# w3's last 64 columns placed directly in front of w4's first 64-row products

## The chip, the cores and the metric

The kernel runs on one core of one Trainium2 chip. The metric is the device time of one execution in microseconds (us), lower is better. A number given for a kernel is the median of several executions; the profile shows one execution, recorded by the hardware profiler.

A core has five engines that run side by side and wait for each other by semaphores: TensorE (PE in the profile; its weight loads are PEld), VectorE (DVE), ScalarE (ACT), GpSimd (POOL) and SyncE (SP, which issues most transfers). Matmul results go to PSUM, which has eight banks of 512 fp32 columns on 128 partitions; ACT and DVE take them out from there. SBUF is the working memory.

## What is computed

Two blocks work on the same input x of 2048 tokens by 640 features, and a gate per token mixes them. Cut to what matters:

```python
x = A_x
g = sigmoid((x * gate_w).sum(-1, keepdims=True))

# A: linear attention with 32 heads of 20, then wo
q, k, v = heads(x @ wqkv)
pq, pk = phi(q), phi(k)                  # phi(t) = where(t > 0, t + 1, exp(t)) + 1e-6
a = ((pq @ (pk.T @ v)) / (pq . sum(pk) + 1e-6)) @ wo

# B: two residual steps
h  = gelu(layernorm(x) @ w1)             # 640 -> 640
hs = shifted(h) @ w2                     # quarters shifted by 1, -1, 2, -2 tokens
x1 = x + hs
h2 = gelu(layernorm(x1) @ w3) @ w4       # 640 -> 1728 -> 640
b  = x1 + h2

out = g * a + (1 - g) * b
```

The change touches the last part, `gelu(layernorm(x1) @ w3) @ w4`. Its inner width is 1728 = 13 x 128 + 64: thirteen full tiles of 128 and a rest of 64.

## The kernel before

**Tiling.** The 2048 tokens are cut into 16 tiles of 128 (`NT`) and 4 chunks of 512 (`NCH`). For w3, a *group* (c, j) makes 128 of the inner columns (j = 0 to 12) for the 512 tokens of chunk c: `w3_group` (line 1076) runs five matmuls of 512 columns over the 640 features into one PSUM bank, and ACT writes the Gelu of it to `h2T`. `h2T` has two slots, so it holds two chunks. Full groups use the whole 128 x 128 array.

The 64 inner columns that are left are made by `w3_half(c)` (line 1085), called for c = 0 and c = 2, each for two chunks. Its weights have 64 columns, so two matmuls run side by side in the two column halves of the array (form 128*64 in the profile): five pairs, one for the even token tiles and one for the odd ones, into the two partition halves of one bank. One Gelu writes the result to `h2h`.

For w4, `w4_half(t)` (line 1146) opens the accumulation of the four token tiles of a chunk with the products of those 64 rows: the rows sit in the two partition halves of `h2h`, so here two matmuls run side by side in the two row halves of the array (form 64*128). There are four of 512 columns (line 1168) and, for the first three chunks, two of 256 (line 1172), which make the last 128 output columns in turned form. It takes six PSUM banks as three pairs and holds them. `w4_turned(t)` (line 1176) then adds the thirteen full tiles to the turned part (line 1188), ACT copies it to `mT`, and a transposing transfer brings it to `mtok`. `w4_tile(t)` (line 1195) adds the thirteen full tiles to the first 512 output columns of one token tile (line 1209), and DVE joins the result with the attention part into `x_tok`. `a_tile(t)` makes that attention part, ten matmuls on a pair of banks.

**The order of the work** is made when the program is built. The work is cut into items; each has a name, a duration, dependencies with a lag, and belongs to a stream, in which items keep their order (`_Items`, line 324). `run` takes, again and again, among the streams' next items whose dependencies are all emitted, the one that can start first by a rough simulation of its own; among equals, items of duration 0 go first (they hold no matmuls of the main line), then the one with the longest chain of durations and lags behind it. The chosen item's function emits its instructions to the queues of the engines, which run in that order on the chip. Waits are derived from what an instruction reads and writes, PSUM by whole banks. A bank is chosen by `bank()` (line 517) or a pair by `pair()` (line 534): the one that has been free longest in the simulation, never one that is held.

**Streams around the change.** Stream W3 holds the groups (c, j) in order of chunk and j. Group (1,7) to (1,10) each wait for an attention tile a(0) to a(3), and a(t) in turn waits for group (1,t+6), so that they alternate. The two items `("w3h", 0)` and `("w3h", 2)` stand in W3 ahead of group (1,11). They need the transposed, normalized x1 of tiles 4 to 7 and 12 to 15 (items t2). Stream W4 holds, for every chunk, w4h, w4x (the turned part, but for the last chunk) and four w4 items; t counts token tiles, so the chunks begin at t = 0, 4, 8 and 12. `("w4h", 0)` depends on a(0), a(3), on w3h(0) and on the last groups of chunks 0 and 1. From t = 4 on, a(t) depends on w4(t-4). Group (2,0) depends on a(7). `KFF` is 13, so `KFF - 2` is j = 11 and `KFF - 1` is j = 12.

On PE the stretch before the change thus runs: a(3), group (1,10), w3h(0), w3h(2), groups (1,11) and (1,12), w4h(0), w4x(0), w4(0), a(4), w4(1), a(5), and so on.

Of the kernel before, what the change touches and what calls it, by code (L numbers as in the profile page):

```python
# [18 lines left out]
KFF = F // 128  # L19
# [397 lines left out]
def _build(nc, A_x, A_wqkv, A_wo, B_w1, B_w2, B_w3, B_w4, gate_w, out, dbg=None, stop=None):  # L417
# [57 lines left out]
    w3 = pa.alloc("w3", [128, KD, F], BF16)  # L475
# [41 lines left out]
    def bank():  # L517
        best = None
        for k_ in range(nbanks[0]):
            b = (bank_rr[0] + k_) % nbanks[0]  # L520
            if b in bank_pend or b in bank_hold:
                continue
            lk = sch.locks.get(b)
            tfree = 0.0 if lk is None else sch.ev_time.get((lk[1].sem, lk[1].val), 1e18)
            if best is None or tfree < best[0]:
                best = (tfree, b)
        bank_rr[0] = best[1] + 1
        bank_pend.add(best[1])
        return best[1]
# [67 lines left out]
    def mm_group(out_ap, pairs, reads_extra=()):  # L597
        n = len(pairs)

        def fn(e, out_ap=out_ap, pairs=pairs, n=n):  # L600
            ins = None
            for i, (l, r) in enumerate(pairs):
                ins = e.matmul(out_ap, l, r, start=(i == 0), stop=(i == n - 1))  # L603
            return ins
        reads = [a for p in pairs for a in p] + list(reads_extra)
        return pe(fn, reads, [out_ap], cost=n * (max(nfree(pairs[0][1]), 24) * 0.4167 + 2.5))
# [39 lines left out]
    def activation(out_ap, in_ap, func, scale=1.0, bias=0.0, accum=None):  # L646
        rd = [in_ap] + [a for a in (scale, bias) if not isinstance(a, (int, float))]
        wr = [out_ap] + ([accum] if accum is not None else [])
        n = nfree(out_ap)
        cost = max(150.0, 100.0 + 0.833 * n + (70.0 if in_psum(in_ap) else 0.0)) + 45.0 * (len(rd) - 1)  # L650
        if accum is not None:
            cost += 91.0
        st_ = ACT_SET.get(func)
        if st_ is not None and st_ != sch.act_func:
            cost += 1290.0
            sch.act_func = st_
        if accum is not None:
            return act(lambda e: e.activation(out_ap, in_ap, func, bias=bias, scale=scale, accum_out=accum), rd, wr, cost=cost)  # L658
        return act(lambda e: e.activation(out_ap, in_ap, func, bias=bias, scale=scale), rd, wr, cost=cost)  # L659
# [103 lines left out]
    def tag_set(buf, sl, what):  # L763
        tags[(buf, sl)] = what

    def tag_chk(buf, sl, what):
        assert tags.get((buf, sl)) == what, ("stale ring slot", buf, sl, what, tags.get((buf, sl)))

    IT = _Items()
# [306 lines left out]
    def w3_group(c, j):  # L1076
        cols = slice(512 * c, 512 * (c + 1))
        sl = c % 2
        if j == 0:
            tag_set("h2T", sl, c)  # L1080
        b = bank()
        mm_group(ps[:, b, :], [(w3[:, k, 128 * j:128 * (j + 1)], xnT[:, k, cols]) for k in range(KD)])
        activation(h2T[:, sl, j, :], ps[:, b, :], ACTF.Gelu_apprx_tanh)

    def w3_half(c):
        b = bank()
        jobs = []
        for k in range(KD):
            xv = xnT[:, k, 512 * c:512 * (c + 2)].rearrange("p (n h q) -> p n h q", h=2, q=128)
            for par in range(2):  # L1090
                jobs.append((ps[64 * par:64 * par + 64, b, :], w3[:, k, 128 * KFF:F], xv[:, :, par, :], k == 0, k == KD - 1))

        def fn(e):
            ins = None
            for o, l, r, st, sp in jobs:
                ins = e.matmul(o, l, r, start=st, stop=sp)  # L1096
            return ins
        pe(fn, [w3[:, :, 128 * KFF:F], xnT[:, :, 512 * c:512 * (c + 2)]], [ps[:, b, :]], cost=KD * 218.0 + 200.0)
        activation(h2h[:, c:c + 2, :].rearrange("p c n -> p (c n)"), ps[:, b, :], ACTF.Gelu_apprx_tanh)
# [46 lines left out]
    def w4_half(t):  # L1146
        sl = (t // 4) % 2
        tag_chk("h2T", sl, t // 4)
        b0, b2, bt = pair(), pair(), pair()
        tiles = [((b0, b2)[i // 2] + i % 2, bt + i % 2, 128 * (i // 2)) for i in range(4)]  # L1150
        for i in range(4):
            w4_banks[t + i] = tiles[i]
        bank_hold.update((b0, b0 + 1, b2, b2 + 1, bt, bt + 1))

        turned = t < NT - 4

        def fn(e):
            ins = None
            for pr in range(2):
                for par, tail in ((0, False), (1, False)) if turned else ((0, False), (1, False), (0, True), (1, True)):  # L1160
                    rows = slice(64 * par, 64 * par + 64)
                    bm, bs, q0 = tiles[2 * pr + par]
                    l = h2h[rows, t // 4, 128 * pr:128 * (pr + 1)]
                    if tail:
                        ins = e.matmul(ps[:, bs, q0:q0 + 128], l, w4[rows, KFF, 512:D], start=(pr == 0), stop=False,
                                       skip_group_check=True)
                    else:
                        ins = e.matmul(ps[:, bm, :], l, w4[rows, KFF, 0:512], start=True, stop=False)  # L1168
            if turned:
                for par in range(2):  # L1170
                    rows = slice(64 * par, 64 * par + 64)
                    ins = e.matmul(ps[:, bt + par, 0:256], w4[rows, KFF, 512:D], h2h[rows, t // 4, :], start=True, stop=False)
            return ins
        pe(fn, [h2h[:, t // 4, :], w4[:, KFF, :]], [ps[:, b, :] for b in (b0, b0 + 1, b2, b2 + 1, bt, bt + 1)], cost=760.0)
# [66 lines left out]
    for c in range(NCH):  # L1241
        for j in range(KD):
            deps = [(("t1", u), 0.9) for u in range(4 * c, 4 * c + 4)] if j == 0 else []
# [6 lines left out]
    for t in range(NT):  # L1250
        c = t // 4
        deps = [(("w1", c, KD - 1), GEL)]
# [8 lines left out]
    for u in range(NT):  # L1261
        deps = [(("s2", u // 4), 3.2 + 0.9 * (u % 4))]
# [8 lines left out]
    for c in range(NCH):  # L1271
        for j in range(KFF):
            deps = []
            if c == 0 and j == 0:
                deps0 = [(("kvt", 1), 0.0), (("z", NT - 1), 1.5)]
            else:
                deps0 = []
            if j == 0:
                deps = deps0 + [(("t2", u), 0.9) for u in range(4 * c, 4 * c + 4)]
                deps.append((("w3load",), 0.0))  # L1280
                if c >= 2:
                    deps.append((("a", 4 * c - 1), 0.0))
            if c == 0 and j == 3:
                deps.append((("w2", NT - 1), 0.0))
            if c == 1 and 7 <= j <= 10:
                deps.append((("a", j - 7), 0.0))
            if c == 1 and j == KFF - 2:
                for c2 in (0, 2):
                    IT.add("W3", ("w3h", c2), 1.27, lambda c2=c2: w3_half(c2), [(("t2", u), 0.9) for u in range(4 * c2 + 4, 4 * c2 + 8)])
            IT.add("W3", ("w3", c, j), 1.08, lambda c=c, j=j: w3_group(c, j), deps)  # L1290
    for t in range(NT):
        deps = [(("zb",), 1.0), (("q", max(t, 2)), 2.0)]
        if t < 7:
# [11 lines left out]
    for t in range(NT):  # L1305
        c = t // 4
        deps = [(("qt", t), 3.0), (("w4load",), 0.0), (("m", 1), 1.0), (("mt",), 2.5)]
        if t >= 4:
            deps.append((("w4", t - 4), 0.3))
        else:  # L1310
            deps.append((("w3", 1, t + 6), 0.0))
        IT.add("AT", ("a", t), 1.33, lambda t=t: a_tile(t), deps)
        deps4 = [(("a", t), 0.0), (("w3h", c - c % 2), GEL), (("w3", c, KFF - 1), GEL)]
        if t % 4 == 0:
            deps4.append((("w3", min(c + 1, NCH - 1), KFF - 1), 0.0))
            if t == 0:
                deps4.append((("a", 3), 0.0))
        elif t + 3 < NT:
            deps4.append((("a", t + 3), 0.0))
        if t % 4 == 0:  # L1320
            IT.add("W4", ("w4h", t), 0.76, lambda t=t: w4_half(t), deps=deps4)
            if t < NT - 4:
                IT.add("W4", ("w4x", t), 2.84, lambda t=t: w4_turned(t), deps=deps4)
        IT.add("W4", ("w4", t), 2.8 if t < NT - 4 else 3.5, lambda t=t: w4_tile(t), deps=deps4)
        if t in OUT_AT:
            IT.add("OUT", ("out", t), 0.0, lambda t=t: out_tiles(OUT_AT[t], t + 1), deps=[(("w4", t), 0.0)])
# [48 lines left out]
```

## Time and profile before

| | us |
|---|---|
| median of 4 executions | 261.16 |
| lowest and highest of them | 260.34, 261.64 |
| the profiled execution's own time | 260.34 |
| its span, first to last instruction | 259.1 |
| PE busy in the span | 254.0 (98%) |
| DVE, ACT, POOL busy | 151.4, 109.7, 94.1 |
| PE in the stretch 112 to 148 | 35.79 of 36.00 |
| PE in the stretch 148 to 154, where the moved items are | 6.00 of 6.00 |
| PE in the stretch 154 to 256 | 101.42 of 102.00 |
| granted TensorE clock | 1.00 |

The profiler's span leaves out 1.2 us of the execution's own time. A matmul is recorded with its latency, so the records of consecutive matmuls overlap, and a PE that is busy the whole time can still start its matmuls further apart than it need; that is read from the starts, not from the busy time. Where a line of the profile names a helper (L603 for groups of matmuls, L659 for activations, L642 for DVE's multiply-adds), the tile names beside it tell what it works on: `xnT` with weights is a w3 group, `pqnT` an attention tile.

### The profile page before, as it was taken

The numbers are of one execution on the slowest core, as the hardware profiler recorded it, in microseconds if no ns is written. First come the engines' busy times: TensorE is split into PE (matmuls) and PEld (weight loads), VectorE is DVE, ScalarE is ACT, GpSimd is POOL, SyncE is SP. The second block draws the span as 40 slices with busy tenths as digits, with TensorE's granted clock in tenths as the row PEclk, the third lists the DMA queues.
The fourth block names the chain that finished last, engine by engine and source line by source line (L and its number), as shares of the span: only waits on it lengthen the run. The fifth ranks groups of instructions, "written<-read, shape, count | busy, mean of one in ns | idle before, by whom it ended". The sixth has DMA issues, their size and how long they took to land.

```text
span 259.1 us, 4106 instructions
## 1 busy us (share of the span) xinstructions
PE 254.0 (98%) x1571; PEld 130.9 (51%) x1600; DVE 151.4 (58%) x290; ACT 109.7 (42%) x223; POOL 94.1 (36%) x152
## 2 busy tenths in 40 slices
PE   8999999999999999999999999999999999999996
PEld 4555555554445554555444555444465444645453
DVE  2587877899914999999993403996004410044333
ACT  1396677751356866675854241005510045300000
POOL 5003995969952118767903201222002110012001
DMA  7665889572754798662835651115010020010211
GB/s 215 198 153 146 150 229 159 168 138 43 107 116 91 126 402 277 74 103 51 91 64 111 129 76 20 28 25 152 0 23 0 0 101 3 0 20 3 102 51 51
DMA packets 54308, 25.86 MB, mean 100 GB/s; under 512 B 45669, under 2 KB 52878, under 8 KB 54289
## 3 DMA queue, kind: packets, MB, share of 16 engines
q1 hardware_dynamic: 52112, 21.21, 36.7%
q0 software_dynamic: 1168, 3.28, 5.5%
q10 hardware_dynamic: 1008, 1.11, 1.3%
q8 instruction: 12, 0.20, 0.4%
q14 instruction: 8, 0.06, 0.1%
HBM read 12.04 MB, written 2.62 MB: 57 GB/s over the span
## 4 chain that ended last, share of the span: by engine, by line
PE 94%; DMA 2%; ACT 1%; issue 1%; SPq 0%; DVE 0%
PE ps L603 59%; PE ps L1209 18%; PE ps L805 8%; PE ps L1188 3%; DMA x_tok<-in_A_x_dram 2%; PE ps L898 2%; ACT hsT L659 1%; PE ps L1096 1%; PE ps L1168 1%; SPq L285 0%; PE ps L899 0%; DVE x_tok L642 0%; PE ps L977 0%; PE ps L1006 0%; ACT junk L658 0%
## 5 line engine op out<-in xcount | busy, mean ns | idle before, releaser
L603 PE MATMUL ps<-xnT,w 128*128 128x512 bf16 x348 | 79.9, 379 | 0.5 <-issue 0.2
L659 ACT ACTIVATE h2T<-ps 128x512 bf16<-128x512 f32 x52 | 30.5, 598 | 60.5 <-PE ps L603 60.4
L603 PEld LDWEIGHTS ps<-xnT,w 128*128 128x128 bf16 x360 | 34.2, 98 | 38.5 <-issue 0.7
L625 POOL TENSOR_SCALAR abx<-x_tok,stg 128x640 f32<-128x640 bf16 x16 | 14.8, 928 | 99.4 <-DVE x_tok L642 94.7
L1209 PE MATMUL ps<-w,h2T 128*128 128x512 bf16 (+1 forms) x253 | 49.4, 346 | 0.4
L642 DVE SCALAR_TENSOR_TENSOR x_tok<-ps,stg,abx 128x512 bf16<-128x512 f32 (+1 forms) x20 | 13.3, 670 | 62.1 <-PE ps L1209 62.1
L625 POOL TENSOR_SCALAR xn<-x_tok,st 128x640 bf16<-128x640 bf16 x32 | 35.4, 1114 | 18.1 <-DMA xnT<-xn 17.6
L1209 PEld LDWEIGHTS ps<-w,h2T 128*128 128x128 bf16 x260 | 22.9, 98 | 22.0 <-issue 0.3
L659 ACT ACTIVATE Er<-ps 128x640 bf16<-128x640 f32 x32 | 22.5, 709 | 15.5 <-PE ps L603 8.4
L658 ACT ACTIVATE junk<-x_tok 128x640 bf16<-128x640 bf16 x32 | 23.6, 739 | 3.3 <-DVE x_tok L640 2.8
L603 PE MATMUL ps<-M_sb,pqnT 128*128 128x128 bf16 (+1 forms) x159 | 24.3, 298 | 0.1
L659 ACT ACTIVATE hsT<-ps 128x512 bf16<-128x512 f32 (+1 forms) x32 | 19.0, 594 | 12.1 <-PE ps L603 11.6
L603 PE MATMUL ps<-w,hsT 128*128 128x128 bf16 (+1 forms) x159 | 23.5, 298 | 0.2
L642 DVE SCALAR_TENSOR_TENSOR abx<-ps,stg,abx 128x640 f32<-128x640 f32 x16 | 14.1, 884 | 15.8 <-PE ps L603 8.8
L603 PE MATMUL ps<-wkg,xT 128*128 128x130 bf16 (+1 forms) x138 | 21.1, 298 | 0.1
L603 PEld LDWEIGHTS ps<-M_sb,pqnT 128*128 128x128 bf16 x160 | 13.6, 98 | 13.0
L603 PE MATMUL ps<-wq,xT 128*128 128x128 bf16 (+1 forms) x128 | 19.7, 298 | 0.1
L603 PEld LDWEIGHTS ps<-w,hsT 128*128 128x128 bf16 x160 | 13.3, 98 | 12.3
L805 PE MATMUL ps<-pk_tok,x_tok 128*128 128x512 bf16 x79 | 17.7, 379 | 0.1
L625 DVE TENSOR_SCALAR Er<-Er 128x640 bf16<-128x640 bf16 x32 | 11.7, 364 | 8.0 <-ACT Er L659 7.8
L1125 DVE TENSOR_TENSOR pq_tok<-pq_tok,dnr 128x300 bf16<-128x300 bf16 (+1 forms) x48 | 15.7, 381 | 0.6
L640 DVE SCALAR_TENSOR_TENSOR x_tok<-ps,x_tok 128x640 bf16<-128x640 f32 x16 | 13.1, 820 | 4.4 <-PE ps L603 3.7
(84 smaller groups left out, 251.1 us busy)
## 6 DMA issues: line engine op xcount, KB each, us to landing
w<-in_B_w_dram SPq DMA_DIRECT2D x1, 2160.0 KB, 8.6
w<-in_B_w_dram SPq DMA_DIRECT2D x1, 2080.0 KB, 14.2
out_dram<-x_tok SPq DMA_DIRECT2D x3, 640.0 KB, 3.1
x_tok<-in_A_x_dram SPq DMA_DIRECT2D x2, 640.0 KB, 5.5
w<-in_B_w_dram POOLq DMA_DIRECT2D x8, 160.0 KB, 4.3
x_tok<-in_A_x_dram SPq DMA_DIRECT2D x5, 160.0 KB, 5.4
wv<-in_A_wqkv_dram POOLq DMA_DIRECT2D x1, 800.0 KB, 5.7
wq<-in_A_wqkv_dram ACTq DMA_DIRECT2D x4, 160.0 KB, 4.1
```

The source lines that it names most:

```text
L603: ins = e.matmul(out_ap, l, r, start=(i == 0), stop=(i == n - 1))
L625: return engf(lambda e: e.tensor_scalar(out_ap, in_ap, s1, s2, op0, op1), rd, [out_ap], cost=cost)
L640: return dve(lambda e: e.scalar_tensor_tensor(out_ap, in0, scalar, in1, op0, op1, accum_out=accum), rd, [out_ap, accum], cost=cost + 70.0)
L642: return dve(lambda e: e.scalar_tensor_tensor(out_ap, in0, scalar, in1, op0, op1), rd, [out_ap], cost=cost)
L658: return act(lambda e: e.activation(out_ap, in_ap, func, bias=bias, scale=scale, accum_out=accum), rd, wr, cost=cost)
L659: return act(lambda e: e.activation(out_ap, in_ap, func, bias=bias, scale=scale), rd, wr, cost=cost)
L805: ins = e.matmul(o, l, r, start=(t0 + q_ == 0), stop=(t0 + q_ == NT - 1))
L898: e.matmul(ps[:, b, 0:512], l, w[:, k, 0:512], start=(k == 0), stop=(k == KD - 1))
L1096: ins = e.matmul(o, l, r, start=st, stop=sp)
L1125: dve(lambda e, o=o, i0=i0, i1=i1: e.tensor_tensor(o, i0, i1, ALU.mult), [i0, dnr[:, 1, sd, :]], [o], cost=cost)
L1188: ins = e.matmul(o, l, r, start=False, stop=(i == KFF - 1))
L1209: ins = e.matmul(o, l, r, start=False, stop=(i == KFF - 1), skip_group_check=(n0 > 0))
```

## The change

Groups (1,11) and (1,12) go first, then the two w3h items, and w4h(0) follows them in the same stream. The w3h items get a(3) as a further dependency, w4h(0) keeps that on the load of w4 alone, and what follows in W4 for t = 0 depends on w4h(0). The written durations of w3h change from 1.27 to 1.14. The instructions of the items are the same ones; w4h(4), w4h(8) and w4h(12) stay where they were.

```diff
             if c == 1 and 7 <= j <= 10:
                 deps.append((("a", j - 7), 0.0))
-            if c == 1 and j == KFF - 2:
+            IT.add("W3", ("w3", c, j), 1.08, lambda c=c, j=j: w3_group(c, j), deps)
+            if c == 1 and j == KFF - 1:
                 for c2 in (0, 2):
-                    IT.add("W3", ("w3h", c2), 1.27, lambda c2=c2: w3_half(c2), [(("t2", u), 0.9) for u in range(4 * c2 + 4, 4 * c2 + 8)])
-            IT.add("W3", ("w3", c, j), 1.08, lambda c=c, j=j: w3_group(c, j), deps)
+                    IT.add("W3", ("w3h", c2), 1.14, lambda c2=c2: w3_half(c2), [(("t2", u), 0.9) for u in range(4 * c2 + 4, 4 * c2 + 8)] + [(("a", 3), 0.0)])
+                IT.add("W3", ("w4h", 0), 0.76, lambda: w4_half(0), [(("w4load",), 0.0)])
...
             if t == 0:
-                deps4.append((("a", 3), 0.0))
+                deps4 = [(("w4h", 0), 0.0)]
         elif t + 3 < NT:
             deps4.append((("a", t + 3), 0.0))
         if t % 4 == 0:
-            IT.add("W4", ("w4h", t), 0.76, lambda t=t: w4_half(t), deps=deps4)
+            if t > 0:
+                IT.add("W4", ("w4h", t), 0.76, lambda t=t: w4_half(t), deps=deps4)
             if t < NT - 4:
                 IT.add("W4", ("w4x", t), 2.84, lambda t=t: w4_turned(t), deps=deps4)
```

## The prediction

> **What bounds the kernel now.** I read the page's busy shares first, then the chain of waits in order of time, then the timeline around the moved code, then who waits for the lines concerned.
>
> ```profile
> PE 254.0 (98%) x1571; PEld 130.9 (51%) x1600; DVE 151.4 (58%) x290; ACT 109.7 (42%) x223; POOL 94.1 (36%) x152
> ```
>
> TensorE has work 98% of a span of 259.1 us; no other engine is above 58%. A busy PE isn't yet the bound of this stretch, so the chain, from the place of the change onwards:
>
> ```profile
> 146.16 2.60 PE ps L603 x15
> 148.76 2.28 PE ps L1096 x20
> 151.04 2.27 PE ps L603 x10
> 153.31 0.54 PE ps L1168 x4
> 153.84 0.11 PE ps L1172 x2
> 153.95 2.94 PE ps L1188 x26
> 156.90 0.05 issue
> ...
> 253.46 2.82 PE ps L1209 x13
> 256.28 0.03 issue
> 256.30 1.08 DVE x_tok L642 x2
> ```
>
> The columns are start, length, and what held the chain. L1096 is the two half-column groups, L603 x10 the last two full groups of w3's second chunk, L1168 and L1172 w4's first 64-row products, L1188 the turned w4 products. From 111.86 us to 256.28 us every step of the chain is PE or one of the 0.05 us "issue" steps: no transfer, Gelu or eviction ends last anywhere. So a tenth of a microsecond taken from or given to PE here arrives at the end whole.
>
> Now the same place in the timeline (start, length with the last matmul's latency, engine, operation, count):
>
> ```profile
> 147.52 1.24 PE L603 MATMUL ps<-xnT,w 128*128 128x512 bf16 x5
> 148.69 2.35 PE L1096 MATMUL ps<-xnT,w 128*64 128x512 bf16 x20
> 150.00 0.60 ACT L659 ACTIVATE h2h<-ps 128x512 bf16<-128x512 f32 x1 [0.61 <-PE ps L1096]
> 150.97 2.33 PE L603 MATMUL ps<-xnT,w 128*128 128x512 bf16 x10
> 151.08 0.60 ACT L659 ACTIVATE h2h<-ps 128x512 bf16<-128x512 f32 x1 [0.48 <-PE ps L1096]
> 153.24 0.61 PE L1168 MATMUL ps<-w,h2h 64*128 64x512 bf16 x4
> 153.68 0.27 PE L1172 MATMUL ps<-h2h,w 64*128 64x256 bf16 x2
> 153.88 3.01 PE L1188 MATMUL ps<-h2T,w 128*128 128x256 bf16 x26
> ```
>
> The shape field (128*128, 128*64, 64*128) is the array form; it changes four times here. One matmul is recorded at 0.38 us (0.27 with 256 columns), so a row's last matmul begins that much before the row's end. Start to start across each change: from 147.52+1.24-0.38 = 148.38 to 148.69, 0.31; from 150.66 to 150.97, 0.31; from 152.92 to 153.24, 0.32; from 153.68 to 153.88, 0.20. The steady spacing is 0.216 with 512 columns ((1.24-0.38)/4) and 0.109 with 256 ((3.01-0.27)/25). Each change thus costs 0.09 to 0.10 us.
>
> **What the Trainium skill says.** "TensorEngine Tiling (Array Packing)", Key Properties: a change of tiling mode, not of the tile alone, drains the TensorE. The trace agrees: about 0.1 us at each of the four. "TensorE: Matmul & The Clock Gate", Back-to-back issue gap, has N/2.4 ns + 2.5 for warm matmuls, 216 ns with 512 columns; the trace has 0.216. Neither page tells a change between two partial forms from one to or from the full array, and the trace of before has no such change.
>
> **The change part by part.** Edit one moves both w3h items (10 pairs of matmuls and 2 Gelus in all) from before w3 group (1,11) to after (1,12). The amount of work is the same. Edit two puts w4h(0) (4 + 2 matmuls) right behind them in the same stream, without its former dependencies. None of this issues a DMA, nothing is moved past an item that does, and SP's and POOL's queues stay as they are.
>
> Before: full, half columns, full, half rows, full. After: full, half columns, half rows, full. Priced over the whole pieces: from 148.76 to 153.95 the chain spends 5.20 us. Without changes the pieces would take 10 x 0.216 (pairs) + 10 x 0.216 + 2 x 0.216 + 0.108 = 4.86. The excess of 0.34 holds three changes, 0.11 each; the fourth is in L1188's 2.94 against 26 x 0.109 = 2.83, also 0.11. If the direct change drains once, as every other does, three remain: **-0.11 us**.
>
> The direct change is the unknown. Below: if the two partial forms needed no drain between them, it costs 0 and the gain is 0.22. Above: the dearest change in the trace is the exit from the 64-column group at L977, where the chain shows the usual change and 0.16 of "issue" behind it, some 0.3 in all; that would make it -0.22+0.3 = +0.1. I take 0.11, since half columns to full, full to half rows and half rows to full cost the same.
>
> Waits. w4h(0) now stands behind the groups whose result it reads. On PE the whole matmul stream is queued behind it, so a wait would cost its full length. From the rows above: the first w3h group's fifth and last pair begins at 148.69 + 0.02 (the first pair is that much longer) + 4 x 0.216 = 149.58, its Gelu 0.42 later (150.00), and the Gelu takes 0.60, so h2h of chunks 0 and 1 is ready 1.02 after. The second w3h group follows at once; its last pair begins 5 x 0.216 = 1.08 after, and w4h's first weights 0.31 later, at 1.39. Slack: 0.37 us, with ACT free (the Gelu of (1,12) ends 0.6 earlier by the same count). That Gelu covers nothing else; if it came 0.37 late, PE would begin to stand.
>
> Banks. w4_half takes three of the four pairs of PSUM banks, longest free first. Between a(3) and w4h(0) stand five one-bank groups in both versions: before (1,10), h0, h2, (1,11), (1,12); after (1,10), (1,11), (1,12), h0, h2. Followed through bank() and pair(), the last two share a pair, which is left out in both versions. So w4h doesn't wait for the second w3h's Gelu; it waits for the first, which it reads anyway, and for a(3)'s eviction, which ends at 148.60. a(4), next to use the left-out pair, comes after w4(0), 6 us later.
>
> Other waits get easier or aren't near: w3h reads later transposes of xnT, later than before; the Gelus of (1,11) and (1,12) come two Gelus sooner and are first read by w4(4), over 30 us on. w4's loads were issued near 88 us and landed within 15.
>
> The planner picks among ready items by the longest chain behind them. The durations (1.27 to 1.14, twice) shorten every chain through (1,10) by 0.26 alike. Only the normalizes and transposes of tiles 12 to 15 fall by more, 2.16+0.13 = 2.29 (they feed w3h(2)); at their turns the nearest ready item of their class is over 4 away. After w3h(2) only w4h(0) can go, since a(4) waits for w4(0). I expect the rest of the order unchanged.
>
> Sum: -0.11. The profiled run took 260.34 (span 259.1 and 1.2 around it), so 260.23 for it; that run is the lowest of the four, so against their median of 261.16 I forecast 261.05, -0.04%.
>
> **Rivals.**
> - Direct change as dear as the two it replaces (it passes through the full form inside the array): 261.16. For: no direct change is in the trace. Against: one drain should empty the array for any next form.
> - No drain between partial forms: 261.16-0.22 = 260.94. Against: both kinds use the whole array, so the forms conflict.
> - The other side, slower: w4h waits for the second w3h's Gelu, if the bank pairs fall otherwise than I followed them. That Gelu ends 1.02 after the last pair begins, and a first product comes some 0.04 later (ACT starts 0.04 after a matmul's end at 148.76), at 1.06 instead of 0.31: +0.75-0.11 = +0.64, 261.80. It decides from the moment the wait passes 0.31+0.11 = 0.42. For: five groups rotate through eight banks and w4h wants six at once. Against: pair() takes the longest free.
> - The edit doesn't do what it says: a full-form item slips between and the changes are four again, 261.16. Against: no other stream has a ready item then.
> - The plan moves elsewhere. The chain has one sore place, 108.54 to 111.86, where PE waits for four hsT Gelus and two Squares; two more Gelus in front there, 0.60 each, would cost 1.2 (262.2), two fewer gain as much (259.8). Against: the chains there shift alike.
>
> **How the numbers follow.** A measurement of this kernel can tell about 0.3% (0.8 us) from no change: its four runs lie between 260.34 and 261.64. Chances: one drain less 0.71; as dear as two, or four changes as before, 0.12; no drain 0.05; second Gelu 0.05; plan moved 0.07, either way. The first three lie inside the bound, save for some 0.02 a side of scatter; half of the Gelu case lies beyond it, and all of the plan case. Faster 0.05, same 0.87, slower 0.08. The range is 260.3 to 261.9: the scatter of the runs about 261.05, with the dear Gelu inside.
>
> **What would show it.** Right: the two full groups stand ahead of L1096, L1168 begins 0.31 after L1096's last pair, the stretch from the first half-column matmul's predecessor to L1188 is 0.11 shorter, and PE is unbroken to the end. Wrong: a gap of 0.4 or more at L1168 with an ACT release behind it (the Gelu), a gap with none (a dear change), or PE rows in another order before 146 or after 154 us (the plan).

## The result and the profile after

| | before | changed |
|---|---|---|
| median, us | 260.71 (64 executions) | 260.00 (43 executions) |
| lowest and highest, us | 259.36, 262.28 | 259.24, 262.01 |
| the profiled execution, its span, us | 260.34, 259.1 | 259.94, 258.7 |

The ratio is 0.9978, with a 95% interval from 0.9968 to 0.9988: some 0.6 us less, where 0.11 was forecast, and a median below the range that was given (260.3 to 261.9). The direction is as forecast and the change is within 0.3%; the time and the size have to be explained.

The chain of waits of the changed kernel, in order of time, from the place of the change to its end (start, length, what held the chain):

```profile
145.90 4.76 PE ps L603 x25
150.66 2.28 PE ps L1096 x20
152.94 0.54 PE ps L1168 x4
153.48 0.11 PE ps L1172 x2
153.59 2.94 PE ps L1188 x26
156.53 0.05 issue
...
253.09 2.82 PE ps L1209 x13
255.91 0.02 issue
255.94 1.07 DVE x_tok L642 x2
```

The two full groups now stand ahead of L1096 (25 matmuls in one piece), and L1168 follows L1096 directly. From the start of the x15 piece before (146.16) to the turned products (153.95) were 7.79 us; now, from 145.90 to 153.59, they are 7.69. In these two profiles that is all that the change does. But this stretch began at 146.16 in the one profile and at 145.90 in the other, 0.26 apart, and the last DVE piece at 256.30 and 255.94, 0.36 apart: 0.26 of the 0.36 was there before the first instruction that the change moves.

The timeline of the same place (start, length with the last matmul's latency, engine, operation, count, and in brackets how long the engine had been idle):

```profile
150.59 2.35 PE L1096 MATMUL ps<-xnT,w 128*64 128x512 bf16 x20
151.90 0.60 ACT L659 ACTIVATE h2h<-ps 128x512 bf16<-128x512 f32 x1 [0.61 <-PE ps L1096]
152.87 0.11 PEld L1168 LDWEIGHTS ps<-w,h2h 64*128 64x128 bf16 x4 [0.41 <-ACT h2h L659]
152.87 0.60 PE L1168 MATMUL ps<-w,h2h 64*128 64x512 bf16 x4
152.98 0.60 ACT L659 ACTIVATE h2h<-ps 128x512 bf16<-128x512 f32 x1 [0.48 <-PE ps L1096]
153.52 3.01 PE L1188 MATMUL ps<-h2T,w 128*128 128x256 bf16 x26
```

L1096's last matmul begins at 150.59 + 2.35 - 0.38 = 152.56, and L1168 at 152.87: 0.31, the same step as at every other change of form. The first h2h Gelu ends at 151.90 + 0.60 = 152.50, 0.37 before it is needed. The bracket on the weight load names that Gelu as the last semaphore that it had; its 0.41 is idle time of the weight load, which every change of form has (0.32 to 0.42 at the four of the kernel before), and no matmul is late. The second Gelu ends at 153.58, long after w4's products have begun, and holds none of them.

### The profile page after: what moved, and what is told of

The parts are those of the page before. It is cut to its first block, busy times and chain, and to the rows that moved or that the text cites. A ratio compares the mean times of both kernels' runs of the same rounds, so it can differ in the third digit from the quotient of the medians.

```text
span 258.7 us, 4105 instructions
## 1 busy us (share of the span) xinstructions
PE 254.2 (98%) x1571; PEld 131.6 (51%) x1600; DVE 151.6 (59%) x290; ACT 109.7 (42%) x223; POOL 95.2 (37%) x152
## 4 chain that ended last, share of the span: by engine, by line
PE 97%; ACT 1%; issue 1%; DVE 0%
PE ps L603 59%; PE ps L1209 18%; PE ps L805 8%; PE ps L1188 3%; PE ps L898 2%; PE ps L871 1%; ACT hsT L659 1%; PE ps L1096 1%; PE ps L1168 1%; PE ps L899 1%; PE ps L614 1%; DVE x_tok L642 0%; PE ps L977 0%; PE ps L1006 0%; ACT junk L658 0%
```

## The experiments

**Theory A**: one drain less is all that the change gives, and the rest of the 0.6 us comes from the scatter of executions and from the comparison. **Theory B**: the changed kernel really gains some 0.5 us, in a way that one profile doesn't show: the later place of the half-column groups, or changes of form that cost more than in the profile.

### The kernel before against itself

No edit: the text of the kernel before, timed against the kernel before, in three batches.

> The kernel before, unchanged, timed against itself, for what the comparison gives where nothing differs. Theory A (only the removed change of array form is real, 0.11 us, and the rest of the 0.6 us is scatter of the start and of the sampling): ratio 1.000 within its interval, spread of the single runs about 2.5 us as before, and the profile's PE rows offset from the first profile of before by a few tenths of a microsecond that arise before the first 10 us. Theory B (the changed kernel really gains about 0.6 us): ratio 1.000 with an interval of 0.1% or less, so that 0.998 is clear of it.

> The kernel before against itself a second time. Theory A: a ratio within 0.2% of 1.000, of either sign, as the batches of one and the same program scatter. A comparison that leans to one side by itself: 0.998 again, as in its first comparison with itself.

> The kernel before against itself a third time, in one batch with the changed kernel. Theory A (the comparison itself leans by a tenth of a per cent or more towards the kernel that is compared): below 1.000 again, about 0.9986. Theory C (the two low ratios were chance): on either side of 1.000.

| batch | reference: median (n) | copy: median (n) | ratio, interval |
|---|---|---|---|
| first | 260.31 (43) | 260.10 (14) | 0.9984 (0.9967 to 1.0001) |
| second | 260.55 (19) | 260.16 (14) | 0.9989 (0.9968 to 1.0009) |
| third | 260.16 (35) | 259.96 (14) | 0.9991 (0.9976 to 1.0006) |

Each interval alone holds 1.000, but all three ratios lie below it, 0.9988 on the mean. Over the three batches the 97 executions of the reference have a mean of 260.36 (standard error 0.06) and the 42 of the copies 260.12 (0.09), for one and the same program: 0.24 us apart, with a standard error of 0.10. So the comparison seems to lean by about 0.24 us towards the kernel that is compared. Chance isn't excluded, and why it should lean isn't shown by these runs.

Two expectations were missed in the first batch. Its interval is so wide that 0.998 lies inside it, so this batch alone can't part the theories. And its profile lost 1.3 us after the first 10 us, as the table further down shows, where Theory A had looked for a few tenths before them.

### The changed kernel again

No edit: the changed kernel, in the first and in the third of these batches.

> The changed kernel once more. Theory A: ratio near 0.9996, its interval touching 1.000 or close to it; PE from the first half-column matmul's predecessor to the turned products again 0.10 us shorter than before. Theory B: ratio 0.998 again, its interval clear of 0.9996.

> The changed kernel in the same batch. Theory A: its single runs' median lies 0.1 us below those of the copy of the kernel before in this batch, within a scatter of some 0.2 us, and its ratio 0.0004 below the copy's. Theory B (a gain of 0.4 to 0.6 us): 0.4 us or more below the copy's.

The ratios are 0.9990 (0.9978 to 1.0002) and 0.9995 (0.9981 to 1.0008), with medians of 259.93 (14 executions) and 260.04 (22), beside 260.10 and 259.96 of the copies of before in the same batches: 0.17 below and 0.08 above. All 79 executions of the changed kernel, the first 43 among them, have a mean of 260.10 (0.06), the 42 copies of before 260.12 (0.09). Their difference, 0.02 with a standard error of 0.11, agrees with 0.11 and with none; it doesn't agree with 0.57. Within these two batches alone the 36 executions of the changed kernel lie 0.10 above the 28 of the copies, with a standard error of 0.12. Theory A's point that the changed kernel would come out below the copy each time was missed in the third batch: the scatter is larger than the effect. So the times can't show the gain of 0.11; the profiles show it.

### Four changes of form again, in the new place

The half-column groups go one full group later than in the kernel before (two in the changed kernel), and one full group stays between them and w4's products. The edit is shown against the changed kernel:

```diff
-            IT.add("W3", ("w3", c, j), 1.08, lambda c=c, j=j: w3_group(c, j), deps)
             if c == 1 and j == KFF - 1:
                 for c2 in (0, 2):
...
+            IT.add("W3", ("w3", c, j), 1.08, lambda c=c, j=j: w3_group(c, j), deps)
+            if c == 1 and j == KFF - 1:
                 IT.add("W3", ("w4h", 0), 0.76, lambda: w4_half(0), [(("w4load",), 0.0)])
```

> The half-column groups come one full group later than before and w4's half-row products follow behind one more full group: the order of the changed kernel, but four changes of form again. Theory A: the profile shows four drains, the stretch to the turned products as long as before, ratio 1.000. Theory B in the form that the later place of the half-column groups brings the gain: ratio 0.998 as in the changed kernel. Theory B in the form that a change of form costs far more in executions without a profile: ratio 1.000.

The ratio is 0.9989 (0.9976 to 1.0001), the median 260.11 (22 executions), like the copy of before in that batch (260.10). The times decide nothing here: the interval holds 1.000 and 0.998, and the changed kernel had 259.93. The chain in its profile:

```profile
145.14 3.68 PE ps L603 x20
148.82 2.28 PE ps L1096 x20
151.09 1.19 PE ps L603 x5
152.28 0.54 PE ps L1168 x4
152.82 0.11 PE ps L1172 x2
152.93 2.94 PE ps L1188 x26
```

From 145.14 to 152.93 are 7.79 us, as in the kernel before. In the profile the later place alone gives nothing; the drain comes back with the full group. (Its span, 258.0 us, is the shortest of all profiles here, with a form change more than the changed kernel: a single span says nothing of the change.)

### Twenty-one changes of form

The five half-column pairs of each w3h are set between the five matmuls of a full group, for (1,11) and (1,12), before w4h(0); again against the changed kernel:

```diff
+    def w3_mixed(c, j, ch):
...
+        for k in range(KD):
+            jobs.append((ps[:, b, :], w3[:, k, 128 * j:128 * (j + 1)], xnT[:, k, cols], k == 0, k == KD - 1))
...
+            for par in range(2):
+                jobs.append((ps[64 * par:64 * par + 64, bh, :], w3[:, k, 128 * KFF:F], xv[:, :, par, :], k == 0, k == KD - 1))
```

> Each of the ten half-column pairs is set between two full matmuls of groups (1,11) and (1,12), so that the array changes form 21 times in this stretch instead of 4 (3 in the changed kernel). Theory A, 0.09 to 0.115 us for each change: +1.6 to +2.0 us against before, ratio 1.006 to 1.008, in the profile and in the times alike. Theory B with a change of form that costs 0.5 us or so in executions without a profile: +8 us or more, ratio over 1.03.

The ratio is 1.0054 (1.0035 to 1.0074), the median 261.73 (6 executions), 1.63 above the copy of before. The ratio is a little below the 1.006 that Theory A expected at the least, with an interval that reaches into its range. In its chain L1114 is the mixed groups, L1188 and L1208 what L1168 and L1188 are above:

```profile
146.26 2.60 PE ps L603 x15
148.86 6.48 PE ps L1114 x30
155.34 0.54 PE ps L1188 x4
155.88 0.11 PE ps L1192 x2
155.99 2.94 PE ps L1208 x26
```

From 146.26 to 155.99 are 9.73 us against 7.79: 1.94 for 17 changes more, 0.114 each. In the times it is 1.63 / 17 = 0.10 each. A change of form costs no more without a profile than with one, and the second form of Theory B falls.

### With the start made calm

Forty more warming matmuls of 512 columns stand in front of the main line, in three kernels; they change no result.

```diff
-        steps = [512] * (cols // 512) + [128] * (cols % 512 // 128)
+        steps = [512] * (cols // 512 + (40 if cols == WARM else 0)) + [128] * (cols % 512 // 128)
```

> The kernel before with 40 more warming matmuls of 512 columns ahead of its first transposes (they change no result), so that x, the weights and the array's full pace are all there before the main line starts. Theory A (scatter from the start alone): PE's main line starts some 8 to 10 us later without a wait, the single runs spread far less than the 2 us of before, and from the first k matmul to the end the profile is as long as in the undisturbed runs. Theory B (the spread lies elsewhere): the spread of the single runs stays near 2 us.

> The changed kernel with the same 40 matmuls ahead. Theory A: 0.11 us below the calm kernel before in the profile and, the scatter gone, 0.1 to 0.15 us below it in the medians of the single runs. Theory B (a gain of 0.4 to 0.6 us that the profiles don't show): 0.4 to 0.6 us below it.

> The kernel with half-column pairs set between full matmuls, with the same 40 matmuls ahead. Theory A: 1.94 us above the calm kernel before (8.36 against 6.42 us in the stretch, as its profile without the 40 has it), so 0.114 for each of 17 changes of form more. Theory B: the changes cost more in executions without a profile than in one with, 4 us or more above.

The medians of six executions each are 268.61, 268.64 and 270.34. The mixed kernel lies 1.73 above the calm kernel before, 0.10 for each of the 17 changes, as without the forty matmuls. The changed kernel lies 0.03 above it where Theory A wanted 0.1 below and Theory B 0.4 or more; with single executions from 268.06 to 269.11 and from 268.17 to 269.07, that tells against B and can't tell 0.1 from nothing. Theory A's claim that the start alone makes the scatter fell. In the three calm profiles the first k matmul comes at 18.54 to 18.71, within 0.17 us, against 9.39 to 10.62 with an ordinary start; but the six times of each calm kernel still spread over 0.90 to 1.32 us, and the six of the mixed kernel with an ordinary start spread over 1.06. Two places behind the start where a profile lost time are in the next section.

## Why the prediction was right and why it was wrong

The profiles can be cut at the starts of certain matmuls, as read from the trace. The first column is a time from the start of the profile, each further one the length from the mark before it (us):

| run | first k matmul at | to the last of k | to the last of w2 | to the last of a(3) | to L1188's first | to the last matmul |
|---|---|---|---|---|---|---|
| before | 10.41 | 42.96 | 65.22 | 28.87 | 6.42 | 102.89 |
| changed | 10.16 | 42.95 | 65.23 | 28.87 | 6.32 | 102.89 |
| copy of before, first | 9.55 | 44.26 | 65.23 | 28.87 | 6.42 | 102.89 |
| changed, second | 10.62 | 42.95 | 65.23 | 28.87 | 6.32 | 102.89 |
| one full group between | 9.39 | 42.95 | 65.23 | 28.87 | 6.42 | 102.89 |
| mixed forms | 10.52 | 42.95 | 65.23 | 28.87 | 8.36 | 102.89 |
| copy of before, second | 10.58 | 42.95 | 65.23 | 28.87 | 6.42 | 102.89 |
| calm before | 18.71 | 42.96 | 65.23 | 29.02 | 6.42 | 102.89 |
| calm changed | 18.55 | 42.95 | 65.23 | 28.87 | 6.32 | 102.89 |

- **One drain less, -0.11 us: right.** The stretch to the turned products took 6.422 and takes 6.315 us, 0.107 less, and it is the same in all four profiles of the changed order (a third copy of it, not in the table, has 6.315 too).
- **The direct change costs what any other does: right.** 312, 311 and 311 ns start to start in three profiles of the changed kernel, where full to half rows has 311 and half columns to full 311. So the two rivals with other prices for it fall. The Trainium skill ("TensorEngine Tiling (Array Packing)", Key Properties) says that changing the tiling mode drains the TensorE, and the trace agrees for the direct change too: it takes the 0.31 us of one drain.
- **Slack of 0.37 before w4h: right**, 152.87 - 152.50. The rival of the second Gelu fell: L1168 begins 0.71 before that Gelu ends.
- **Nothing else in the plan moves: right.** The instruction order of PE and ACT differs only in the moved groups, DVE's and SP's not at all, and the rest of PE's stretches agree within 5 ns between the two profiles.
- **The gain arrives whole at the end: right.** The last column is the same in all runs. That the measured time fell by 0.6 us confirms none of this: copies of the unchanged kernel came out lower as well.

**The step that failed** is the last one of the sum, the time that it starts from: "that run is the lowest of the four, so against their median of 261.16 I forecast 261.05". The median of four was taken as if it were sharp, and the range was laid about it. Sixty-four executions of that kernel, those four among them, have a median of 260.71, 0.45 lower. Less 0.11 that would have been 260.60, and a range of the same width about it, from some 259.8 to 261.4, would have held the measured 260.00.

The size is a second matter: by the means of the comparison in the result (64 and 43 executions) the change brings 0.57 us (standard error 0.12), of which the profiles give 0.11 to the drain. What the comparison of the program with itself showed takes 0.24 (0.10). That leaves 0.22, with a standard error of 0.16, so it may be scatter; in the three later batches it didn't return. It lies on the side of the kernel before: its 64 executions have a mean of 260.66, the 97 later ones 260.36, while the changed kernel had 260.09 then and 260.11 later. The cause stays open. The three later batches ran on three different chips, and which chip that comparison ran on isn't known, so a difference between chips isn't excluded. The runs speak against a change of form dearer than 0.12; an effect of the place alone is seen in no profile, and the profiles show no stretch other than the start in which the two kernels differ, besides the one that was changed.

The prediction also passed over what the profile of before showed: its chain began with a transfer of x that held it for 5.41 us, up to 7.61. Where the profiles differ, it is mostly in the start: the first k matmul comes between 9.39 and 10.62 where nothing was put in front. Two rows of the timeline of the kernel before, PE's in the start:

```profile
7.15 0.22 PE L899 MATMUL ps<-wq,xT 128*128 128x128 bf16 x1
7.65 0.45 PE L614 MATMUL ps<-ident,x_tok 128*128 128x128 bf16 x5 [0.28 <-DMA x_tok<-in_A_x_dram]
```

and of the changed kernel:

```profile
7.36 0.22 PE L899 MATMUL ps<-wq,xT 128*128 128x128 bf16 x1
7.41 0.44 PE L614 MATMUL ps<-ident,x_tok 128*128 128x128 bf16 x5
```

The third x tile's transposes (L614) stood idle for 0.28 us in one execution and not in the other; in the second run of the changed kernel it was 0.66. A later place is shown by the first copy of before, whose k stage is 1.3 us longer than any other:

```profile
40.59 0.43 PE L805 MATMUL ps<-x_tok,pk_tok 128*128 128x512 bf16 x2
42.11 1.53 PE L603 MATMUL ps<-wq,xT 128*128 128x512 bf16 x10 [1.09 <-DMA xT<-x_tok]
```

There a transposing transfer of x landed late in one execution. The calm kernel before has 0.15 us more than the others from the last of w2 to the last of a(3), where a weight load of w3 waited 0.15 us for DVE's `x_tok`. None of this has to do with the change, and each such event is larger than its 0.107 us.

## What to carry to other kernels

Count the changes of array form in a tuned matmul stream and price each from the trace, 0.107 to 0.114 us here. Setting groups of two different partial forms side by side saved one of them here; the operand of the second has to be ready in time, which it was by 0.37 us. Before a gain of a thousandth is claimed or denied, time the old kernel against its own copy, and cut the two profiles at the same instructions: here most stretches agreed to a few nanoseconds, while whole executions of one program differed by up to 2.9 us. And a forecast of a time needs the scatter of the number that it starts from, not only of the step that is added.

## What wasn't expected of the hardware

The pace of the matmuls doubles at a different moment in different executions. The timeline of the changed kernel, 512-column matmuls (L898) followed by 128-column ones (L899), start first:

```profile
5.49 0.63 PE L898 MATMUL ps<-wq,xT 128*128 128x512 bf16 x1
5.91 0.31 PE L899 MATMUL ps<-wq,xT 128*128 128x128 bf16 x1
6.02 0.63 PE L898 MATMUL ps<-wq,xT 128*128 128x512 bf16 x1
6.45 0.31 PE L899 MATMUL ps<-wq,xT 128*128 128x128 bf16 x1
6.55 0.42 PE L898 MATMUL ps<-wq,xT 128*128 128x512 bf16 x1
6.81 0.22 PE L899 MATMUL ps<-wq,xT 128*128 128x128 bf16 x1
```

and of the kernel with one full group between:

```profile
4.38 0.38 PE L898 MATMUL ps<-wq,xT 128*128 128x512 bf16 x1
4.59 0.22 PE L899 MATMUL ps<-wq,xT 128*128 128x128 bf16 x1
```

From a 512-column matmul to the next start are 0.42 or 0.43 us up to 6.45 in the first, and 0.21 from 4.38 on in the second, though the first matmul comes at 0.83 in both; the profile gives the granted clock as 1.00 in both. The Trainium skill ("TensorE: Matmul & The Clock Gate", Part 1) says that the array starts at half its pace and that the window after which it is released runs freely, so that the moment varies; these traces agree in both. It puts the variation at 500 ns to either side; here the two moments lie over 2 us apart. This is one part of the 1.2 us by which the first k matmul differs between programs whose starts are the same, the transfer of x above another.
